# More of layer 1 by seven products: three units of group 7 and four of group 8 in an attention and squared-ReLU kernel

## The chip, the cores and the metric

The kernel runs on one core of a Trainium2 chip. A core has a matrix engine (TensorE, PE in the profile; its weight loads are listed apart as PEld), a vector engine (VectorE, DVE), a scalar engine (ScalarE, ACT), a general engine (GpSimd, POOL) and SyncE (SP), which here only issues DMA transfers. Operands lie in the on-chip memory in 128 partitions; matmul results lie in PSUM, of which this kernel uses eight banks of 128 x 512 fp32. The metric is the time of one execution in microseconds (us) on the device. The page and the trace show one profiled execution.

## The reference

First an attention with a relative position bias, for 8 batches of 8 heads, 576 positions of 64 numbers:

```
scores = scale * q @ k^T + bias_table[bucket(|i - j|)]   # scale = 1/8
attn   = exp(scores - max) ; attn /= sum(attn) + 1e-9
out    = attn @ v
```

Its output, 4608 tokens of 512 numbers (heads side by side), goes through two layers:

```
h   = maximum(x @ w_in, 0)       # w_in: 512 x 2048
out = (h * h) @ w_out            # w_out: 2048 x 512
```

Inputs and output are fp32. The kernel computes in fp16 with fp32 sums.

## The kernel before

**Staging.** Heads are worked in pairs, 32 in all (pair 4b + hp is batch b, heads 2hp and 2hp + 1). GpSimd issues casting loads of q and k into a ring of five staging buffers (`load_six`, `load_rows`). For the first two batches TensorE transposes them; from batch 2 on SyncE issues DMA transposes into `qt` and `kt` (L910). TensorE makes the scores (`run`, L971), ScalarE their exponentials into one of three buffers `pt` (L984), VectorE multiplies the part near the diagonal by exp(bias) (L710), TensorE multiplies by v (`values`, L736 and L743, into the one PSUM bank of `r_pv`), VectorE normalises into `x` (L757, L762), and `x` is transposed into `xt`, from batch 2 on again by SyncE's DMA (L777).

**The two layers** run on 9 groups (0 to 8) of 512 tokens. Layer 1 of a group has 16 tiles of 128 columns of w_in; a plain tile is four matmuls with 512 columns (`f1`, L1486), a ReLU out of PSUM on ScalarE (L1515) and a square on VectorE into `g` (L1525). Layer 2 (`second`) always goes by seven products of quarter blocks in place of eight: sums of activations (`sums_of_activations`, L1170) and of weights are made beforehand, the products are matmuls with 256 columns (L1215, eight for each half of a product), and the quarters of the output are put together on ScalarE and VectorE (L1249, L1243) and stored by SyncE (L1271). In the instruction stream layer 2 of group g - 1 is laid between layer 1 of group g; at the end layer 2 of group 8 stands alone.

**Layer 1 by sevens.** `by_sevens(g, units, due)` does some of the tiles of groups 7 and 8 in the same manner. One unit u takes four tiles (two of each half of w_in's columns) in seven products in place of eight. Four sums of blocks of `xt` are made once for a group, in staging buffers (`t`, names `qs` and `ks` in the profile). For each unit four sums of blocks of w_in are made, 128 x 512 each (`late_sums`, L1296), and serve both groups. They lie in a buffer of the exponentials, `late["room"]`, taken from the ring of three once the last pair's scores are made. A product is four matmuls with 256 columns (L1370). Its results go through PSUM banks a and d (those of the scores, `r_set`), b (`r_g`) and c (the values' one bank, `r_pv`), where products 5 and 3 of a unit share c. Product 1 is copied out by ScalarE (L1401), products 6, 5, 7, 3 and 4 by an add on VectorE (L1396), product 2 goes through the ReLU straight from the bank (L1401); the other three finished quarters get their ReLU in place (L1410), and all four a square on ScalarE or VectorE (L1419, L1421). Before, `UNITS` gives group 7 one unit and group 8 two, so 12 and 8 tiles stay plain.

**What sets the order.** No engine is programmed directly. `P.add` collects operations with their engines, dependencies, buffers and a due time; `Plan.schedule` then simulates the engines with estimated costs, and of the operations that can start first on an engine it takes the one with the earliest due time. The order so found is the order of each engine's instructions. Engines then run in order and wait on semaphores. The table `DUES` overrides the due times of single operations, by their number in the order of `P.add`. A due time is a priority in the planner's nanoseconds, and the profile's clock runs otherwise. Operations that matter below: 98 is the load of pair 5's q; 240, 242 and 244 are the three loads of pair 15's k, and SyncE's transposition into `kt` waits for all three; 1118 and 1094 are the first two plain tiles of group 2, which wait for `xt` of pairs 8 to 11; 1178 is a run of scores of pair 12, 1229 the second part of pair 13's values; 2033 and 2035 are scores of pair 28. From 2150 on numbers differ between the two kernels, since `by_sevens` makes other numbers of operations.

Of the kernel before, what the change touches and what calls it, by code (L numbers as in the profile page):

```python
# [40 lines left out]
SIX = 2  # L41
V_EARLY, V_HW = 18900.0, 2
LATE2 = 7000
UNITS = {7: 1, 8: 2}
V_AFTER = 8
HALVES, HSTEP, HL1 = 1, 1650.0, (20000.0, 34000.0)

AT = (0, 0.5, 2, 2.5, 4, 5.5, 7)
# [15 lines left out]


DUES = """
0:6314 10:217026 16:13035 20:13348 21:258484 25:16976 56:-3806 60:10549 64:7807 66:10391 72:10797 74:9599
80:12958 82:13335 86:9426 88:22059 90:20784 96:15474 98:18110 100:27635 102:17069 104:20413 106:19133 108:15929
110:20294 112:11373 114:26373 118:23163 120:26863 122:27399 124:27420 126:43949 128:373644 130:37551 132:55933
140:51535 146:53249 148:57194 150:58550 152:59093 154:59407 156:62212 158:60024 162:61598 164:73576 166:62626  # L70
168:69684 170:59456 172:62632 174:65227 176:55548 182:127159 185:61268 197:113382 198:91426 200:94475 202:78241
204:62718 208:77636 228:78221 232:79984 234:88997 236:93444 258:97082 260:107098 264:95693 272:353255 290:132179
294:109389 312:161034 317:126634 462:185572 468:197791 498:216177 504:216419 528:-11357 540:58268 548:290781
552:-273 556:362102 569:117287 570:18693 572:322613 573:269880 577:216286 580:63789 588:19830 590:16140
594:14836 595:13461 604:192461 605:259149 615:250357 618:40193 621:36476 626:164336 627:19259 631:22289
632:61824 637:27216 640:23193 641:22984 642:25439 646:24359 648:23862 654:35487 655:137994 656:25970 657:147534
658:26859 669:32802 670:29693 671:29115 675:26812 678:61416 684:27758 687:32723 692:45873 693:44475 694:33461
700:29155 703:40767 706:43870 707:156896 712:138157 715:49177 721:51431 727:42451 730:41204 733:51304 736:188811
739:160633 741:60556 745:65841 746:65543 750:23359 752:198955 754:252034 755:87356 757:149452 759:161491
764:165691 772:38120 780:31226 786:44132 789:65256 791:41900 794:47703 798:179998 803:183900 804:201524  # L80
806:29768 808:32093 814:128297 817:38985 819:48235 822:13166 831:74297 834:41254 836:42214 847:56558 872:76658
876:81357 881:86779 885:82175 890:132194 892:78033 896:74640 901:77029 905:85179 910:92737 913:136934 921:-441
928:71969 932:86010 949:99012 964:77998 968:82501 971:73188 973:72043 979:88379 993:74328 994:172863 1011:91462
1016:95167 1034:90187 1037:94214 1061:98210 1066:103404 1085:116705 1089:123193 1094:115422 1098:123870
1105:125413 1109:116922 1114:123206 1117:104913 1118:108524 1126:215561 1127:140015 1134:341379 1138:129625
1149:123522 1156:126934 1159:128458 1174:117297 1178:116128 1183:123079 1184:121785 1193:130123 1197:131687
1210:103421 1213:171180 1215:111597 1218:107124 1224:123395 1234:97893 1238:106935 1239:113870 1242:121817
1245:107498 1247:139583 1250:140247 1256:140312 1264:152762 1302:164129 1307:159578 1311:156509 1314:140955
1322:175554 1327:174839 1336:155878 1340:158933 1342:162590 1347:179715 1351:176523 1358:154680 1362:174863
1365:164726 1369:178450 1372:164377 1375:183307 1391:148354 1396:141354 1405:158959 1423:158387 1426:145359  # L90
1428:154083 1460:162604 1493:305936 1511:188689 1515:208724 1518:185439 1520:203719 1524:203903 1527:183718
1531:64671 1534:35571 1535:192349 1540:192734 1544:215992 1547:197129 1549:206804 1552:201055 1553:198295
1560:216382 1567:22170 1571:213455 1575:214781 1579:220037 1582:216714 1585:209292 1589:218699 1604:51306
1609:177927 1612:165312 1615:244855 1616:185704 1636:180272 1639:191978 1641:180694 1668:199141 1673:209138
1676:207232 1684:113822 1687:219314 1700:201270 1701:203032 1703:191761 1708:195625 1724:230338 1733:225496
1736:226874 1737:226114 1740:65884 1747:238275 1753:233568 1762:229606 1766:238797 1773:230961 1777:231038
1784:245369 1788:237869 1795:246877 1798:236767 1817:211479 1818:211996 1836:232334 1849:219048 1852:216620
1854:244560 1857:216881 1881:227052 1884:224715 1886:230825 1887:234567 1889:218551 1895:248220 1896:246247
1916:239890 1932:255715 1937:245391 1946:276466 1950:271723 1957:144182 1961:262946 1966:264120 1969:283402
1970:252823 1973:283834 1975:263020 1986:281169 1997:277541 2001:273225 2008:269557 2011:263820 2030:290375  # L100
2033:300439 2035:288262 2038:298147 2070:215597 2094:283860 2099:280265 2140:278987 2160:322023 2175:327834
2187:203430 2191:314100 2194:95297 2196:320960 2200:327640 2205:312307 2209:311170 2216:306662 2220:44915
2227:316413 2231:323176 2238:310309 2241:322560 2256:323083 2258:322318 2260:298171 2281:330645 2283:323528
2290:323454 2298:283980 2316:319108 2342:324427 2349:318937
"""


# [156 lines left out]
def kernel(  # L264
# [48 lines left out]
    pts, p4s = ([t[:, i, :] for i in range(NPT)] for t in (pt_sb, pm_sb))  # L313
# [22 lines left out]
    r_qk, r_pt, r_x = Ring(NQK, True), Ring(NPT), Ring(NX)  # L336
# [28 lines left out]
    def load(*args, **kw):  # L365
# [29 lines left out]
        due=5,  # L395
# [237 lines left out]
    l_win, l_wout, i_wout = [], [], []  # L633
# [55 lines left out]
    last_scores = []  # L689
# [595 lines left out]
    late = {}  # L1285

    def sum_of_w(i, u):
        return pts[late["room"].slot][:, ts(i - 1, 1024)].rearrange("p (k c) -> p k c", k=2)[:, :, ts(u, 256)]

    def late_sums(n, dst, terms, deps, due, bufs=()):  # L1290

        o, made_ = None, []
        for i, (a, b_, op) in terms:
            o = P.add(
                {"DVE": dve(n, 2.0)},
                lambda i=i, a=a, b_=b_, op=op: io(nc.vector.tensor_tensor(out=dst(i), in0=a(), in1=b_(), op=op)),  # L1296
                deps + [o], bufs, due,
            )
            made_.append(o)
        return made_  # L1300
# [2 lines left out]

    def by_sevens(g, units, due):

        assert max(UNITS.values()) <= 2
        if not late:

            late["room"] = Buf(r_pt)
        c = (g * GT) % XR  # L1310
        assert c + GT <= XR
        wq = lambda i, k, u: w_in_sb[:, 2 * k : 2 * k + 2, 1024 * i + 256 * u : 1024 * i + 256 * u + 256]
        xq = lambda k, j: xt_sb[:, 2 * k : 2 * k + 2, c + HALF * j : c + HALF * j + HALF]
        o_ = 4 * (g - min(UNITS)) - 1
        t = lambda i: stg[(i + o_) // 2][(i + o_) % 2][:, 0:512].rearrange("p (k c) -> p k c", k=2)
# [10 lines left out]
        gb1 = g_bufs[g]  # L1326
        for u in range(units):
            s_ = lambda i, u=u: sum_of_w(i, u)
            if ("ops", u) not in late:
                late["ops", u] = late_sums(  # L1330
                    512, s_,
                    [
                        (1, (lambda u=u: wq(1, 0, u), lambda u=u: wq(1, 1, u), mybir.AluOpType.add)),
                        (2, (lambda s_=s_: s_(1), lambda u=u: wq(0, 0, u), SUB)),
                        (4, (lambda u=u: wq(0, 1, u), lambda s_=s_: s_(2), SUB)),
                        (3, (lambda u=u: wq(0, 0, u), lambda u=u: wq(1, 0, u), SUB)),
                    ],
                    l_win + last_scores, due + 10.0 * u, [late["room"]],
                )
            banks = {"a": Buf(r_set), "b": Buf(r_g), "c": Buf(r_pv), "d": Buf(r_set)}  # L1340
            y = {"u": Buf(r_f), "v": Buf(r_y)}
# [16 lines left out]
            for n, i in enumerate((1, 6, 2, 5, 7, 3, 4)):  # L1358
                bk, left, right, first_ = prod[i]
                st = banks[bk]  # L1360
# [5 lines left out]
                def mul(left=left, right=right, first_=first_, ps=ps):  # L1366
# [9 lines left out]
                o = P.add(  # L1376
                    {"PE": 4 * mm(HALF)}, mul,
                    xt_ready[g] + t_ops + late["ops", u] + (read_of[after_read[i]] if i in after_read else []),
                    [st, gb1, late["room"]], due + (8 * u + AT[n]) * 2000.0, 0.0, "f",
                )  # L1380
                f1_last.setdefault(g, []).append(o)
                to, plus, where = reads[i]
# [82 lines left out]
    def layers(g):  # L1465
# [4 lines left out]
        if g < NG:  # L1470
            g_bufs[g] = Buf(r_gb)
            gb1 = g_bufs[g]
            squares[g] = {nt: [] for nt in range(16)}
            units = UNITS.get(g, 0)
            if g < HALVES:
# [82 lines left out]
    for x in DUES.split():  # L1558
        i, due = x.split(":")
# [34 lines left out]
```

## Time and profile before

| what | value |
|---|---|
| five runs | 368.93, 365.24, 367.34, 366.69, 367.06 us |
| median | 367.06 us |
| the profiled execution | 368.93 us, its span 367.1 us |
| matmuls | 4062, of them 84 in units by sevens |
| first matmul, last engine work | 5.3 us, 364.4 us |
| transfers | 44.29 MB, mean 121 GB/s |

In the profile's lines `f<-xt,w_in_sb` means a result tile and its operands, `x16` a count, `L1486` a line of the kernel. A group's line gives the busy time, the mean of one in ns, and after the bar the idle time of the engine before it with what ended it. A line of the chain gives its start, its length and what ran. A stretch gives its length and then the busy time of PE, PEld, DVE, ACT and POOL, with the granted clock of TensorE, the share of the DMA engines and GB/s. In a list of instructions in order of time, start and length come first, and an idle time before the instruction stands in brackets with its releaser. TensorE's granted clock was 1.00 in all stretches.

### The profile page before, as it was taken

How to read it: one execution, taken by the hardware profiler on the slowest of the kernel's cores; microseconds unless marked ns; L12 is line 12 of the kernel's file. 1: busy time of each engine (PE TensorE's matmuls, PEld its weight loads, DVE VectorE, ACT ScalarE, POOL GpSimd, SP SyncE). 2: the span in 40 equal slices, each digit the busy share in tenths (PEclk: the TensorE clock that was granted, in tenths of full speed). 3: DMA queues.
4: the chain of work that ended last, by engine and by line, in shares of the span. 5: the costliest groups of instructions: out<-in, count | busy, mean ns of one | idle time of the engine just before them, and what ended most of it. 6: DMA issues, size and time to landing. Idle time of an engine off the chain costs nothing.

```text
span 367.1 us, 10232 instructions
## 1 busy us (share of the span) xinstructions
PE 353.7 (96%) x4062; PEld 253.0 (69%) x4062; DVE 269.9 (74%) x622; ACT 260.3 (71%) x385; POOL 188.4 (51%) x345
## 2 busy tenths in 40 slices
PE   3989999999999799999999999999999999999996
PEld 3658787765687357777776666557777788566885
DVE  4888989768965499558596579557767785589683
ACT  4999997488866598688977787883685751567530
POOL 8888389989968869978669755013000000000000
PEclk9999999999999999999999999999999999999999
DMA  9999999999999999999999979125320122000032
GB/s 169 139 149 201 202 168 178 134 173 189 119 134 151 220 132 177 149 187 139 155 125 164 177 130 103 63 52 82 105 63 3 49 77 75 31 29 2 30 114 89
DMA packets 162256, 44.29 MB, mean 121 GB/s; under 512 B 145664, under 2 KB 162208, under 8 KB 162208
## 3 DMA queue, kind: packets, MB, share of 16 engines
q0 software_dynamic: 74208, 14.53, 53.0%
q1 hardware_dynamic: 87696, 28.80, 44.8%
q8 instruction: 32, 0.52, 0.6%
q10 hardware_dynamic: 304, 0.31, 0.3%
q14 instruction: 16, 0.13, 0.1%
HBM read 36.89 MB, written 9.44 MB: 126 GB/s over the span
## 4 chain that ended last, share of the span: by engine, by line
PE 85%; DMA 7%; ACT 3%; issue 2%; DVE 2%; POOL 0%; ACTq 0%; SPq 0%
PE f L1215 28%; PE f L1486 26%; PE pv L743 9%; PE st L971 7%; PE f L1439 4%; PE pv L736 3%; DMA xt<-x 2%; DMA kt<-ks 2%; PE st L997 2%; PE st L1022 2%; DMA qs<-in_q_dram 2%; PE st L1370 1%; DMA g<-c_rep 1%; PE f L927 1%; ACT rt L1515 1%
## 5 line engine op out<-in xcount | busy, mean ns | idle before, releaser
L984 ACT ACTIVATE pt<-st 128x1024 f16<-128x1024 f32 x112 | 108.6, 1023 | 25.2 <-PE st L971 25.2
L1486 PE MATMUL f<-xt,w_in_sb 128*128 128x512 f16 (+4 forms) x592 | 113.9, 333 | 2.1 <-DMA xt<-x 2.1
L1515 ACT ACTIVATE rt<-f 128x512 f16<-128x512 f32 x116 | 68.2, 606 | 34.5 <-PE f L1486 31.2
L1486 PEld LDWEIGHTS <-w_in_sb 128*128 128x128 f16 x592 | 51.8, 98 | 44.6 <-issue 12.1
L710 DVE TENSOR_TENSOR pt<-pt,tb_sb 128x512 f16<-128x512 f16 (+3 forms) x108 | 61.6, 583 | 18.1 <-ACT pt L984 16.8
L1525 DVE TENSOR_TENSOR g<-rt 128x512 f16<-128x512 f16 x116 | 51.3, 448 | 28.6 <-ACT rt L1515 27.1
L1215 PEld LDWEIGHTS <-g 128*128 128x128 f16 x576 | 54.6, 98 | 9.0 <-issue 2.1
L349 POOL DMA_DIRECT2D ks<-in_k_dram x79 | 55.9, 720 | 7.2 <-DMA kt<-ks 3.9
L349 POOL DMA_DIRECT2D qs<-in_q_dram x79 | 55.5, 712 | 4.1 <-DMA qt<-qs 2.7
L743 PE MATMUL pv<-va,pt 128*128 128x65 f16 x1280 | 54.6, 193 | 0.0
L743 PEld LDWEIGHTS <-pt 128*128 128x128 f16 x1280 | 50.2, 97 | 2.6 <-issue 0.6
L1215 PEld LDWEIGHTS <-s 128*128 128x128 f16 x432 | 40.9, 98 | 9.4 <-issue 4.2
L1243 DVE SCALAR_TENSOR_TENSOR y<-f,y 128x512 f32<-128x512 f32 (+1 forms) x47 | 31.3, 666 | 18.6 <-PE f L1215 16.4
L1215 PE MATMUL f<-wt,g 128*128 128x256 f16 x288 | 36.2, 273 | 0.0
L954 POOL COPY qz<-qt 64x64 f16<-64x64 f16 x56 | 17.9, 319 | 35.2 <-DMA qt<-qs 30.0
L736 PE MATMUL pv<-vm,pm 128*128 128x130 f16 x160 | 35.4, 221 | 0.4 <-DVE x L762 0.4
L1215 PE MATMUL f<-w_out_sb,s 128*128 128x256 f16 x288 | 35.8, 273 | 0.0
L971 PE MATMUL st<-qt,kt 64*128 64x512 f16 x224 | 33.9, 381 | 0.1
L1215 PE MATMUL f<-w_out_sb,g 128*128 128x256 f16 x272 | 33.3, 273 | 0.0
L762 DVE TENSOR_TENSOR x<-pv,r 128x384 f16<-128x384 f32 (+1 forms) x64 | 31.1, 486 | 1.1
L954 POOL COPY qz<-kt 64x64 f16<-64x64 f16 x56 | 21.1, 376 | 10.4 <-DMA kt<-ks 4.5
L1170 DVE TENSOR_TENSOR s<-g,s 128x1024 f16<-128x1024 f16 x36 | 24.6, 687 | 0.1
(101 smaller groups left out, 410.9 us busy)
## 6 DMA issues: line engine op xcount, KB each, us to landing
out_dram<-y SPq DMA_DIRECT2D x34, 256.0 KB, 2.7
f<-in_v_dram SPq DMA_DIRECT2D x24, 256.0 KB, 4.7
ks<-in_k_dram POOLq DMA_DIRECT2D x48, 64.0 KB, 5.1
qs<-in_q_dram POOLq DMA_DIRECT2D x48, 64.0 KB, 4.5
w_in_sb<-in_moe_w_in_dram POOLq DMA_DIRECT2D x4, 512.0 KB, 8.9
w_out_sb<-in_moe_w_out_dram POOLq DMA_DIRECT2D x4, 512.0 KB, 12.8
ks<-in_k_dram POOLq DMA_DIRECT2D x7, 144.0 KB, 4.8
qs<-in_q_dram POOLq DMA_DIRECT2D x7, 144.0 KB, 5.5
```

What stands on the lines that cost most here:

```text
L349: lambda: io(eng.dma_start(out=out_(), in_=in_())),
L710: io(nc.vector.tensor_tensor(out=a, in0=a, in1=t, op=MULT))
L736: nc.tensor.matmul(ps[:, i, :, :], pm[:, c : c + 128], vm[:, hp, :, 0:65], start=True, stop=False)
L743: nc.tensor.matmul(ps[:, i, e, :], pt[:, (2 * jt + e) * S + c : (2 * jt + e) * S + c + 128], va[:, jt, 2 * hp + e, 0:65], start=False, sto ...
L954: io(eng.tensor_copy(out=dst[qb.slot][rw, rw], in_=src[qb.slot][rw, 512:576]))
L971: nc.tensor.matmul(sets_ps[st.slot][:, e, :], kt[rw, ts(jt, 128)], qt[rw, 0:512], start=True, stop=True,)
L984: nc.scalar.activation(out=p5(pts[pb.slot])[:, jt, :, 0:512], in_=sets_ps[st.slot], func=EXPF, scale=SCALE)
L1215: nc.tensor.matmul(home[bf.slot][:, ts(s_, HALF)], left(c, s_), right(c), start=(c == 0 and (s_ == 0 or apart) and (own or i not in before ...
L1243: nc.vector.scalar_tensor_tensor(out=dst, in0=ps, scalar=OSC, in1=ys[y[plus].slot][:, cs], op0=MULT, op1=mybir.AluOpType.add,)
L1486: nc.tensor.matmul(g_ps[bank.slot][:, a:z], w_in_sb[:, kk, ts(nt, 128)], xt_sb[:, kk, c : c + z - a], start=(kk == 0), stop=(kk == 3),)
L1515: io(nc.scalar.activation(out=rts[rb.slot], in_=g_ps[bank.slot], func=RELUF))
L1525: nc.vector.tensor_tensor(out=gs[gb1.slot][:, nt, :], in0=rts[rb.slot], in1=rts[rb.slot], op=MULT)
```

## The change

`UNITS` becomes 3 for group 7 and 4 for group 8. Group 7 keeps 4 plain tiles, group 8 none. Since a buffer of the exponentials has room for the sums of two units, `by_sevens` takes a second one for units 2 and 3; each unit's sums and products name the room of its pair of units. The sums of units 0, 1 and 2 are now made in group 7's call, those of unit 3 in group 8's. The table of due times is replaced whole: 369 entries before, 407 after, 271 numbers in both.

```diff
-UNITS = {7: 1, 8: 2}
+UNITS = {7: 3, 8: 4}
...
-80:12958 82:13335 86:9426 88:22059 90:20784 96:15474 98:18110 100:27635 102:17069 104:20413 106:19133 108:15929
...
-204:62718 208:77636 228:78221 232:79984 234:88997 236:93444 258:97082 260:107098 264:95693 272:353255 290:132179
...
-1016:95167 1034:90187 1037:94214 1061:98210 1066:103404 1085:116705 1089:123193 1094:115422 1098:123870
-1105:125413 1109:116922 1114:123206 1117:104913 1118:108524 1126:215561 1127:140015 1134:341379 1138:129625
-1149:123522 1156:126934 1159:128458 1174:117297 1178:116128 1183:123079 1184:121785 1193:130123 1197:131687
...
-2033:300439 2035:288262 2038:298147 2070:215597 2094:283860 2099:280265 2140:278987 2160:322023 2175:327834
...
+62:2550 64:8438 66:10313 72:11673 74:9688 80:13143 82:13878 86:9063 88:22768 90:22033 96:14893 98:16878
+100:27518 102:16143 104:21298 106:19938 108:15518 110:20673 112:12408 114:24018 118:23393 120:25313 122:26048
...
+224:80823 226:82118 232:80198 238:89360 240:102185 248:79548 272:114280 280:100590 315:105196 380:132130
...
+1089:120669 1094:116281 1098:124916 1105:126024 1106:127920 1108:102699 1109:118659 1114:121637 1117:105997
+1118:115418 1127:131252 1137:111596 1145:133367 1148:113447 1149:123947 1152:114544 1156:127111 1159:129421
+1178:117144 1183:123401 1184:125052 1186:114321 1197:132662 1206:94845 1210:103572 1215:111049 1218:106871
+1224:122501 1229:119522 1243:120869 1247:137326 1250:140324 1256:144888 1302:162213 1307:160803 1311:157524
...
+2011:265340 2033:262802 2035:268045 2044:275820 2076:261902 2094:280562 2097:270160 2099:277583 2102:275597
...
     def sum_of_w(i, u):
-        return pts[late["room"].slot][:, ts(i - 1, 1024)].rearrange("p (k c) -> p k c", k=2)[:, :, ts(u, 256)]
+        room = pts[late["room", u // 2].slot][:, ts(i - 1, 1024)]
+        return room.rearrange("p (k c) -> p k c", k=2)[:, :, ts(u % 2, 256)]
...
     def by_sevens(g, units, due):
 
-        assert max(UNITS.values()) <= 2
-        if not late:
-
-            late["room"] = Buf(r_pt)
+        for u in range(units):
+            if ("room", u // 2) not in late:
+                late["room", u // 2] = Buf(r_pt)
...
-                    l_win + last_scores, due + 10.0 * u, [late["room"]],
+                    l_win + last_scores, due + 10.0 * u, [late["room", u // 2]],
...
-                    [st, gb1, late["room"]], due + (8 * u + AT[n]) * 2000.0, 0.0, "f",
+                    [st, gb1, late["room", u // 2]], due + (8 * u + AT[n]) * 2000.0, 0.0, "f",
```

## The prediction

> **What bounds the kernel now.** I read the page first (busy time, then the chain that ended last), then the busy time in stretches, the chain in the last 65 us, the groups of the vector and scalar engines there, and at the end the waits of TensorE and SyncE's queue.
>
> ```profile
> PE 353.7 (96%) x4062; PEld 253.0 (69%) x4062; DVE 269.9 (74%) x622; ACT 260.3 (71%) x385; POOL 188.4 (51%) x345
> PE 85%; DMA 7%; ACT 3%; issue 2%; DVE 2%; POOL 0%; ACTq 0%; SPq 0%
> 120.00:140.00 20.00, 18.47 (x159) 9.35 (x159) 14.08 (x33) 16.54 (x26) 15.37 (x27) 1.00 1.46 179
> 270.00:310.00 40.00, 40.00 (x467) 31.41 (x466) 28.48 (x65) 22.78 (x32) 0.00 (x0) 1.00 0.17 46
> 310.00:348.00 38.00, 38.00 (x273) 26.42 (x271) 28.55 (x58) 23.31 (x42) 0.00 (x0) 1.00 0.09 29
> ```
>
> TensorE is the bound: 85% of the chain, and not idle at all from 140 us until its last matmul. The third and fourth numbers of a stretch are PE and PEld, the next two the vector engine (DVE) and the scalar engine (ACT). In 310 to 348 us, where groups 7 and 8 do the layer 1 that the change touches, DVE has 9.5 us free and ACT 14.7. The 1.5 us missing in 120 to 140 us belong to a wait that is shown below. So time comes off the end only as matmuls go away, or as one of TensorE's few waits does.
>
> ```profile
> 313.05 1.73 PE f L1486 x8
> 330.38 0.87 PE st L1370 x8
> L1370 PEld LDWEIGHTS <-pt x48: 97/98/98, 318.7 to 347.9; 128*128 128x128 f16 x48
> L1515 ACT ACTIVATE rt<-f 128x512 f16<-128x512 f32 x20 | 11.8, 595 | 15.4 <-PE f L1486 14.3 <-DVE g L1525 0.7 <-DVE y L1396 0.3
> L1525 DVE TENSOR_TENSOR g<-rt 128x512 f16<-128x512 f16 x20 | 8.3, 422 | 6.0 <-ACT rt L1515 5.7
> L1396 DVE SCALAR_TENSOR_TENSOR rt<-st,y 128x512 f16<-128x512 f32 x3 | 2.1, 686 | 0.0
> L1401 ACT ACTIVATE f<-st 128x512 f32<-128x512 f32 x3 | 1.8, 590 | 0.0
> L1410 ACT ACTIVATE rt<-rt 128x512 f16<-128x512 f16 x7 | 4.4, 623 | 2.7 <-DVE rt L1396 2.7
> L1419 ACT ACTIVATE g<-rt 128x512 f16<-128x512 f16 x7 | 4.4, 630 | 0.2
> L1296 DVE TENSOR_TENSOR pt<-w_in_sb x4: 395/417/419, 272.8 to 280.4; 128x512 f16<-128x512 f16 x4
> ```
>
> **The change, part by part.** The sums go against the profiled execution: 368.93 us, its span of 367.1 and 1.8 around it. That is 1.9 above the median of the five runs (367.06), so I apply the same differences to the median.
>
> *Matmuls.* A plain unit is four tiles of four 512-column matmuls: 16 at 1.73/8 = 0.216 us, 3.46 us. By sevens it is 28 matmuls of 256 columns at 0.87/8 = 0.109: 3.05 us. Four more units: 4 x 0.41 = 1.66 us less on TensorE, all on the path, since nothing else bounds it there. That the smaller matmul pays for its weights is excluded by the third line above: a load takes 98 ns, the matmuls still start 109 ns apart, so loads run under matmuls.
>
> Here a rule speaks against the change. The Trainium skill (TensorE: Matmul & The Clock Gate, "The mechanism") lists that a weight load overlaps matmuls in flight only where the row group differs; these loads all take the full 128 rows. By that rule the 12 more loads of a unit would stand open, 12 x 98 ns, 4.7 us for four units, and the change would lose 3.0. The row above disagrees (the same section also speaks of a background weight buffer), and I go by the row.
>
> *Evictions.* Each unit drops four ReLUs (0.595, ACT) and four squares (0.422, DVE). It adds on DVE five adds at 0.686 (3.43 us), on ACT one copy 0.590, one ReLU from the bank 0.60 and three in place at 0.623 (3.06), and four squares on either engine (0.63 or 0.42). For four units in 300 to 350 us: DVE goes from 35.9 busy (the sum of its ten-microsecond stretches) by -6.8 and +13.7 to 42.8 without squares and 49.6 with all 16; ACT from 25.7 by -9.5 and +12.2 to 28.4, or 38.5 with all squares. The stretch shrinks to 48.3. So if ACT takes most squares (it took seven of ten in this stage) both fit and the cost is 0; if DVE took all, it would be 1.3 over. Ends 0 and +1.3. I take +0.2, near the first, by that share and because back-to-back adds start closer than they last (347.45, 348.06, 348.65 us).
>
> *Sums of w_in.* Units 2 and 3 need eight more sums of 0.417, 3.3 us on DVE. The stretch 270 to 310 leaves DVE 11.5 us, and their room, a second exponentials' buffer, is free once a pair's values are done. Cost 0; without that cover they would stand before the first products of unit 2 and cost up to 3.3. Unit 1's sums only move from group 8's call to group 7's.
>
> *The end of layer 1.* The last product of group 8 goes matmul, add, ReLU, square, and then group 8's layer 2 may start. Before, the last product began at 347.63, its square ended at 351.24 and layer 2 began at 351.56, with 0.3 to spare, TensorE busy with group 7's layer 2 meanwhile. With four units in a row two or three such chains queue. Ends 0 (cover kept) and +1.4 (two more adds of 0.69 in front). I take +0.2, near the row.
>
> *The table of due times.* It is new from end to end. Set against the order in which the trace has the same operations (those below 2150 are the same in both kernels), most new entries repeat that order; up to some 60 us nearly all queues stand as before. The last batch's attention is reordered: pair 28's scores (2033, 2035) get 262802 and 268045 for 300439 and 288262, so values that ran at 301 to 306 us come some 20 us sooner. TensorE is full on both sides of that move, so it costs nothing; it frees the exponentials' buffers sooner and takes normalising off DVE in the last stage.
>
> One place is not neutral:
>
> ```profile
> 116.41 0.60 PE L971 MATMUL st<-qt,kt 64*128 64x512 f16 x4
> 118.14 0.22 PE L736 MATMUL pv<-vm,pm 128*128 128x130 f16 x1
> 118.66 0.81 PE L1486 MATMUL f<-xt,w_in_sb 128*128 128x512 f16 x3
> 121.53 2.75 PE L1486 MATMUL f<-xt,w_in_sb 128*128 128x512 f16 x12 [2.06 <-DMA xt<-x]
> 110.01 1.22 SPq L910 DMA_TRANSPOSE kt<-ks  x1
> 111.94 2.90 SPq L777 DMA_TRANSPOSE xt<-x  x2
> 113.63 7.86 DMA xt<-x
> ```
>
> TensorE waits 2.06 us for the transposed activations of pair 11, which sit on SyncE's queue behind pair 15's k and take 7.86 us to land. The new table puts a score (1178) and values (1229) that ran just before, 0.54 and 0.60, behind the first of these tiles (1118: 115418, against 117144 and 119522): if the transfer lands as before, TensorE arrives 1.14 earlier and waits that much more. But it also puts one load of pair 15's k (240) from the head of the queue to 102185 (it was issued at 83.5 us); then the k transposition is not ready at its old place, the activations go ahead of it, 1.3 us sooner (1.22 and its gap), and pair 15's scores at 130 us have time. Arrival 1.14 earlier and landing 1.3 to 2 earlier nearly cancel. Ends -2.06 (the wait gone) and +1.14. I take -0.3, nearest to the cancelling.
>
> Here the Trainium skill (DMA: Bandwidth & Descriptors, "Issuing engines are not separate DMA queues") says that transfers of all issuing engines share the same 16 DMA engines. The run agrees: q0 and q1 together fill 97.8% of them. So a landing also moves with every load that the table shifts, and the ends stay in the range.
>
> In the first 40 us four GpSimd loads stand 0.3 to 0.6 us earlier by the table, one of them (98) the load for which TensorE waits 0.61 us at 24.12. Ends -0.6 and +0.6 (as much later); I take 0.
>
> **Sum.** -1.66 + 0.2 + 0.2 - 0.3 = -1.56: 367.4 for the profiled execution, 365.5 for the median.
>
> **Rivals.**
> 1. *The gain is waited away at 121 us.* The transfer lands as before: -1.66 + 1.14 + 0.4 = -0.1, 366.9. For it: the row, and that its neighbours landed late too (the k transposition 4.2, the v load between them 7.1 us after issue). Against: the moved k load.
> 2. *The values' one bank bounds the last stage; slower.* Products 5 and 3 of each unit share it, from product 5's start to the end of product 3's add. In before it was held from 344.14 to 349.33, 5.2 us, and 333.25 to some 339.4, 6.1. Seven holds now go one after another into about 38 us: from 5.4 us each it decides. At 5.8 it gives 40.6 - 38 = 2.6 us more than before, 369.7. For it: the third hold, on a busy DVE, was 5.2. Against: the parts alone are 0.44 + 0.69 twice, and the first unit's 13 us was no need but order.
> 3. *Waits go too.* The wait at 121 us and that at 24 vanish: -1.66 - 2.06 - 0.6 + 0.4 = -3.9, 363.1. For it: both loads are moved the right way. Against: DMA is near full there.
>
> **How the numbers follow.** Forecast 0.50, own range 364.3 to 366.8 (+/-1.2 from the terms' ends). Rival 1 0.20, rival 2 0.14, rival 3 0.13, rest 0.03. Half a per cent, 1.84 us, is about what this kernel's runs can tell from nothing (they spread from 365.24 to 368.93); it lies at 365.22. Faster beyond it: half of the forecast's 0.50 less a little (0.22), rival 3 (0.13), a little of rival 1 (0.03): 0.38. Slower: rival 2 and some rest, 0.16. Same: 0.46. The range leaves out most of rival 3's far side and of rival 2's: 363.8 to 368.9.
>
> **What would show it.** Right: L1486's 512-column matmuls fall by 64 and L1370's rise from 84 to 196, at 109 ns; TensorE without idle from 140 us to its end; layer 2 of group 8 starting 1.3 to 2 us sooner. The wait for xt near 121 us tells the forecast from rivals 1 and 3. Wrong: idle TensorE in 310 to 350 us released by L1396 or L1421, or the last matmuls of group 8's layer 2 no sooner than before.

## The result and the profile after

The changed kernel takes 365.49 us (median of 45 runs, 363.44 to 368.05), the kernel before 366.38 (median of 87, 364.89 to 369.17). The ratio is 0.9974, with a 95% interval of 0.9963 to 0.9985: 0.95 us faster (0.55 to 1.36), a gain that is real and lies inside the half per cent that the prediction called "same". The forecast of 365.5 us met the time itself. But it was reached by taking 1.56 from 367.06, and that median of five runs stood 0.7 above the median of 87: so the right time is in part luck, and of the difference 0.6 us is missing. The rest of this document is about where it went.

One caution for reading traces: the profiled execution of before (368.93 us) was 2.5 us above its median, that of after (365.40) is close to its own. Their difference is not the change's.

First the busy time and the chain of after, from the page:

```profile
PE 351.2 (97%) x4110; PEld 256.9 (71%) x4110; DVE 279.5 (77%) x642; ACT 268.2 (74%) x399; POOL 188.1 (52%) x343
PE 84%; DMA 5%; POOL 4%; ACT 3%; DVE 3%; issue 2%; SPq 0%
```

The matmuls are 48 more (64 of 512 columns gone, 112 of 256 come), TensorE's busy time is 2.5 us less, and GpSimd, which was at 0% of the chain, is at 4%. The stretches of after, with the columns as before (length, PE, PEld, DVE, ACT, POOL, granted clock, DMA share, GB/s):

```profile
120.00:140.00 20.00, 20.00 (x209) 11.30 (x208) 15.92 (x38) 17.90 (x28) 14.76 (x27) 1.00 1.68 169
180.00:200.00 20.00, 19.18 (x233) 13.22 (x232) 16.35 (x37) 14.96 (x22) 16.83 (x31) 1.00 1.72 150
270.00:310.00 40.00, 40.00 (x449) 31.66 (x447) 32.20 (x77) 21.87 (x35) 0.00 (x0) 1.00 0.18 50
310.00:348.00 38.00, 38.00 (x346) 33.67 (x345) 33.61 (x58) 30.29 (x54) 0.00 (x0) 1.00 0.11 36
```

The idle time at 120 to 140 us is gone. The stages of the last 160 us keep TensorE full, with VectorE now at 33.6 of 38 us where it was at 28.6. And a stretch that the prediction never looked at, 180 to 200 us, has 0.8 us of idle TensorE.

The end of layer 1 in after, from the lists of instructions of VectorE and TensorE:

```profile
344.13 0.68 DVE L1400 SCALAR_TENSOR_TENSOR rt<-pv,f 128x512 f16<-128x512 f32 x1
344.73 1.28 DVE L1400 SCALAR_TENSOR_TENSOR rt<-st,f 128x512 f16<-128x512 f32 x2
347.18 0.41 DVE L1425 TENSOR_TENSOR g<-rt 128x512 f16<-128x512 f16 x1
348.12 1.91 PE L1219 MATMUL f<-w_out_sb,g 128*128 128x256 f16 x16
```

The last square ends at 347.59 and layer 2 of group 8 begins at 348.12, 0.5 us later and with TensorE busy on group 7 in between. Lines of the changed kernel are four higher than before (L1486 is L1490, L954 is L958).

The place of the new loss, first TensorE's list of after, then GpSimd's:

```profile
193.66 1.46 PE L1490 MATMUL f<-xt,w_in_sb 128*128 128x512 f16 x6
195.49 0.42 PE L1026 MATMUL st<-qt,qz 128*128 128x288 f16 x2 [0.37 <-POOL qz L958]
196.36 0.38 PE L1001 MATMUL st<-qz,kt 128*128 128x128 f16 x4 [0.45 <-DMA f<-in_v_dram]
```

```profile
188.54 2.13 POOL L353 DMA_DIRECT2D ks<-in_k_dram  x3
190.71 0.23 POOL L958 COPY qz<-kt 64x64 f16<-64x64 f16 x1
190.88 2.11 POOL L353 DMA_DIRECT2D qs<-in_q_dram  x3
192.96 2.14 POOL L353 DMA_DIRECT2D ks<-in_k_dram  x3
195.15 0.29 POOL L958 COPY qz<-kt 64x64 f16<-64x64 f16 x1
195.49 0.81 POOL L958 COPY qz<-qt 64x64 f16<-64x64 f16 x2
196.36 0.62 POOL L958 COPY qz<-kt 64x64 f16<-64x64 f16 x2
```

Two pieces of scores wait on `qz`, small copies of `qt` and `kt` that GpSimd makes (L958), 0.82 us in all. They stand behind six load issues, 0.71 us each, 190.88 to 195.10. The second wait carries the name of a load of v; the two `qz` copies before it were done at 196.30 (195.49 and 0.81), so it is those that it waited for, as a run below confirms. In before the same copies stood ahead of their loads, on GpSimd:

```profile
192.37 0.23 POOL L954 COPY qz<-kt 64x64 f16<-64x64 f16 x1
192.66 0.51 POOL L954 COPY qz<-qt 64x64 f16<-64x64 f16 x2
193.21 0.51 POOL L954 COPY qz<-kt 64x64 f16<-64x64 f16 x2
193.78 0.23 POOL L954 COPY qz<-qt 64x64 f16<-64x64 f16 x1
193.95 2.12 POOL L349 DMA_DIRECT2D qs<-in_q_dram  x3
```

The old table holds back two load operations there, 462 with due time 185572 and 468 with 197791. The new table has no entry for either. That became the theory: the units and the last stage give all that was forecast, or a little more, and the two lost entries give about 1 us back at 195 us. The rivals: the units themselves give less (evictions, the end of layer 1, the values' bank), or the new table is worse in some other place.

### The profile page after: what moved, and what is told of

Its sections match the earlier page's. It is cut to its first block, busy times and chain, and to the rows that moved or that the text cites. A ratio compares the mean times of both kernels' runs of the same rounds, so it can differ in the third digit from the quotient of the medians.

```text
span 363.6 us, 10367 instructions
## 1 busy us (share of the span) xinstructions
PE 351.2 (97%) x4110; PEld 256.9 (71%) x4110; DVE 279.5 (77%) x642; ACT 268.2 (74%) x399; POOL 188.1 (52%) x343
## 4 chain that ended last, share of the span: by engine, by line
PE 84%; DMA 5%; POOL 4%; ACT 3%; DVE 3%; issue 2%; SPq 0%
PE f L1219 29%; PE f L1490 21%; PE pv L747 9%; PE st L975 7%; PE f L1443 4%; PE st L1374 3%; PE pv L740 3%; DMA va<-in_v_dram 2%; PE pv L1374 2%; PE st L1026 2%; PE st L1001 2%; POOL va L353 1%; DMA f<-in_v_dram 1%; DMA g<-in_k_dram 1%; ACT pt L988 1%
## 5 line engine op out<-in xcount | busy, mean ns | idle before, releaser
L1490 PE MATMUL f<-xt,w_in_sb 128*128 128x512 f16 (+4 forms) x528 | 98.3, 328 | 0.0
L1519 ACT ACTIVATE rt<-f 128x512 f16<-128x512 f32 x100 | 58.6, 610 | 21.1 <-PE f L1490 18.6
L1490 PEld LDWEIGHTS <-w_in_sb 128*128 128x128 f16 x528 | 45.6, 98 | 36.5 <-issue 8.9
L1529 DVE TENSOR_TENSOR g<-rt 128x512 f16<-128x512 f16 x100 | 42.4, 433 | 19.7 <-ACT rt L1519 18.4
L958 POOL COPY qz<-qt 64x64 f16<-64x64 f16 x57 | 20.1, 352 | 35.0 <-DMA qt<-qs 20.7
L761 DVE RECIPROCAL r<-pv 128x6 f32<-128x6 f32 (+1 forms) x64 | 11.8, 184 | 16.9 <-PE pv L747 16.2
```

The costliest lines, as they stand in the source:

```text
L1490: nc.tensor.matmul(g_ps[bank.slot][:, a:z], w_in_sb[:, kk, ts(nt, 128)], xt_sb[:, kk, c : c + z - a], start=(kk == 0), stop=(kk == 3),)
L1519: io(nc.scalar.activation(out=rts[rb.slot], in_=g_ps[bank.slot], func=RELUF))
L1529: nc.vector.tensor_tensor(out=gs[gb1.slot][:, nt, :], in0=rts[rb.slot], in1=rts[rb.slot], op=MULT)
```

## Experiments

Each ratio is to the kernel before, timed beside it on the same chip.

**Units with the old table up to the last stage.** The changed kernel, but operations below 1300 have their old due times (462 and 468 among them), the rest the new ones.

```diff
-62:2550 64:8438 66:10313 72:11673 74:9688 80:13143 82:13878 86:9063 88:22768 90:22033 96:14893 98:16878
...
+82:13335 86:9426 88:22059 90:20784 96:15474 98:18110 100:27635 102:17069 104:20413 106:19133 108:15929 110:20294
...
+312:161034 317:126634 462:185572 468:197791 498:216177 504:216419 528:-11357 540:58268 548:290781 552:-273
...
```

> The changed kernel (three and four units) with the new table from operation 1300 on, and the old table below, so that the first 120 us and GpSimd's loads stand as in the kernel before. Theory: the matmuls give their whole 1.6 us and nothing is waited away in the last stage; TensorE waits for xt near 121 us as before, and the new wait near 195 us (scores behind copies on GpSimd) is gone: 1.6 us faster than before, ratio 0.9956. Rival (the units themselves give only what the changed kernel shows, the rest goes to adds and ReLUs in the last stage): 0.9 us faster, ratio 0.9975.

Measured: 364.58 us against 366.46, ratio 0.9933 (0.9907 to 0.9960). The rival's 0.9975 is excluded: the loss is not in the units or the last stage. There is no wait at 195 us, and none at 121 us either, where the theory expected that of the kernel before.

**The new table alone.** The kernel before, units 1 and 2, with the new due times for all operations below 2150.

```diff
...
-1105:125413 1109:116922 1114:123206 1117:104913 1118:108524 1126:215561 1127:140015 1134:341379 1138:129625
...
+226:82118 232:80198 238:89360 240:102185 248:79548 272:114280 280:100590 315:105196 380:132130 528:34973 539:46297
...
+1105:126024 1106:127920 1108:102699 1109:118659 1114:121637 1117:105997 1118:115417 1127:131252 1137:111596
...
```

> The kernel before (one and two units) with the new due times for all operations below 2150. TensorE's work is that of before. Theory: the wait for xt near 121 us goes and a wait of about 1 us near 195 us comes; where the first is as long in most executions as in the profiled one, 1.0 us faster (0.9973); where it is usually short, up to 0.7 us slower (1.002), which is what the sum of units and table must give to make the 0.95 us measured. Rival (the table does nothing for the time): 0.9995 to 1.0005.

Measured: 366.96 against 366.46, ratio 1.0015 (0.9995 to 1.0035). If anything the table costs time (0.55 us, -0.2 to 1.3), the second of the two cases that the theory allowed. Its trace has no wait at 121 us and has the wait for `qz` again; of TensorE's waits in this kernel:

```profile
PE f L1486 <- DMA xt<-x: 0.7, 1, 0.7
PE st L997 <- DMA f<-in_v_dram: 0.4, 1, 0.4
PE st L997 <- POOL qz L954: 0.2, 1, 0.2
```

Columns: total us, times, longest. The first is at 157 us and does not stand in the changed kernel's trace.

**The copies ahead of the loads.** The changed kernel with five instructions placed elsewhere in the order and nothing else; 474 is the first load operation of the second group of six issues.

```diff
-    for op in P.schedule():
+    order = P.schedule()
+    moved = [P.ops[i] for i in [1667, 1696, 1697, 1698, 1699]]
+    order = [op for op in order if op not in moved]
+    at = order.index(P.ops[474]) + 0
+    order[at:at] = moved
+    for op in order:
```

> The changed kernel with five copies into qz and kz on GpSimd (operations 1667 and 1696 to 1699, for the scores that TensorE waits for near 195 us) put ahead of six load issues instead of behind them; nothing else moves. Theory: the two waits at 195.5 and 196.4 us go, 1.0 us faster than the changed kernel, 1.9 faster than before, ratio 0.9947. Rival (those waits are of the profiled execution only, or the next late thing takes their place): as the changed kernel, 0.9974.

Measured: 364.51 against 366.46, ratio 0.9935 (0.9910 to 0.9961), an interval that lies wholly below that of the changed kernel. In its list for GpSimd the copies are made at 189.57 and TensorE has its scores at 195.28 without a wait:

```profile
187.42 2.10 POOL L353 DMA_DIRECT2D ks<-in_k_dram  x3
189.57 0.62 POOL L958 COPY qz<-kt 64x64 f16<-64x64 f16 x2
190.25 0.72 POOL L958 COPY qz<-qt 64x64 f16<-64x64 f16 x2
191.03 0.51 POOL L958 COPY qz<-kt 64x64 f16<-64x64 f16 x2
191.48 2.11 POOL L353 DMA_DIRECT2D qs<-in_q_dram  x3
195.28 0.41 PE L1026 MATMUL st<-qt,qz 128*128 128x288 f16 x2
```

**The two entries put back.** The changed kernel with two more entries in its table.

```diff
...
-224:80823 226:82118 232:80198 238:89360 240:102185 248:79548 272:114280 280:100590 315:105196 380:132130
-528:34973 539:46297 540:53567 543:58725 548:8583 556:10502 560:11253 569:15224 570:13674 572:18408 576:8662
...
+226:82118 232:80198 238:89360 240:102185 248:79548 272:114280 280:100590 315:105196 380:132130 462:185572
+468:197791 528:34973 539:46297 540:53567 543:58725 548:8583 556:10502 560:11253 569:15224 570:13674 572:18408
...
```

> The changed kernel with two entries of the old table put back (462:185572 and 468:197791, two loads of q and k on GpSimd that the old table held back and the new one does not). Nothing else in the table moves. Theory: these two entries are what kept the copies ahead of the loads; the waits at 195 to 196 us go, and the time is that of the run with the copies ahead, 1.0 us faster than the changed kernel, ratio to before 0.9947. Rival (it needs the copies themselves moved): as the changed kernel, 0.9974.

Measured: 364.51 against 366.40, ratio 0.9935 (0.9912 to 0.9958); no wait at 195 us. So both repairs of the same place, by order and by due time, give the same 1.0 us by the medians (1.4 by the ratios); the idle time that the trace of the changed kernel showed there was 0.82. Both beat both kernels.

**The table with the two entries, without the units.** The second experiment plus 462 and 468; the one line of the table in which the two differ is shown. With it all four corners of units and entries are measured. (The "fifth experiment" of its expectation is the run with the two entries put back.)

```diff
-226:82118 232:80198 238:89360 240:102185 248:79548 272:114280 280:100590 315:105196 380:132130 528:34973 539:46297
+226:82118 232:80198 238:89360 240:102185 248:79548 272:114280 280:100590 315:105196 380:132130 462:185572 468:197791 528:34973 539:46297
```

> The kernel before (one unit and two) with the new table for operations below 2150 and the two entries 462 and 468 put back, so that the second experiment and this one differ in these two entries alone, and this one and the fifth experiment in the units and the last stage. Theory (units and entries add: units -1.9 us, the two missing entries +0.5 to +1.0, all else in the table 0): 365.9 to 366.5 us, ratio to before 0.999 to 1.001, 0.5 to 1.0 us faster than the second experiment, and no wait for the rearranged copies near 195 us. Rival (other entries of the new table gain or lose as well, and hide in the units' figure): the ratio lies beyond 0.9975 or 1.0025.

Measured: 365.82 against 366.29, ratio 0.9985 (0.9972 to 0.9998). No wait at 195 us. The four corners:

| ratio to before | entries missing | entries there |
|---|---|---|
| one unit and two | 1.0015 (0.9995 to 1.0035) | 0.9985 (0.9972 to 0.9998) |
| three units and four | 0.9974 (0.9963 to 0.9985) | 0.9935 (0.9912 to 0.9958) |

Times 366.4 us and with the half-widths added in squares: the missing entries cost 1.1 +/- 0.9 us with few units and 1.4 +/- 0.9 with many; the units with the last stage give 1.5 +/- 0.8 and 1.8 +/- 1.0; what is left of the new table gives 0.55 (0.1 to 1.0). Along one edge, -0.55 + 1.1 - 1.5 = -0.95, the result. The theory missed narrowly, always to the faster side: 365.82 where 365.9 to 366.5 was expected, 0.9985 where 0.999 to 1.001 was, 1.1 us from the second experiment where 0.5 to 1.0 was. So its statement that all else in the table is worth 0 did not quite hold; the rival's bound, 0.9975, was not reached either.

**Is the gain at 121 us the transfer's?** The prediction's step there was that the transposition of pair 15's k goes behind `xt`. This kernel is before with that one instruction moved on SyncE's queue.

```diff
+    moved = [P.ops[i] for i in [1268]]
+    order = [op for op in order if op not in moved]
+    at = order.index(P.ops[1078]) + 1
+    order[at:at] = moved
```

> The kernel before with one instruction moved: SyncE's transposition of pair 15's k (operation 1268) behind the transposition of pair 11's activations (1078). Theory: the activations are issued about 1.3 us sooner and land sooner by as much, TensorE's wait near 121 us falls from 2.1 to 0.8 us or less, 0.5 to 1.3 us faster, ratio 0.9965 to 0.9986. Rival (the landing is set by the full DMA engines, not by the place in the queue): the wait stays, ratio 1.000.

Measured: 366.47 against 366.46, ratio 1.0005 (0.9980 to 1.0030). In its list for SyncE's queue, and TensorE's:

```profile
109.94 2.58 SPq L777 DMA_TRANSPOSE xt<-x  x2
119.44 3.62 PE L1486 MATMUL f<-xt,w_in_sb 128*128 128x512 f16 x16
```

The second of the two was issued at 111.26 and landed at 115.80, and no wait is left at the tiles. The mechanism is there and the time isn't: the interval leaves at most 0.7 us for it. The rival's ratio came, without its reason, since the wait did not stay.

**Before once more.** The same kernel, unchanged, profiled a second time.

> The kernel before, unchanged, for a second profile. Theory (the 2.1 us wait for xt near 121 us belongs to the slow execution that was profiled first, 368.93 us): no wait of over 0.5 us there, span near 364.6. Rival (the wait is usual, and the moved transposition failed to remove it): 1 to 2.5 us again.

Measured: 367.18 us in one run. From its lists:

```profile
111.77 2.60 SPq L777 DMA_TRANSPOSE xt<-x  x2
119.34 3.62 PE L1486 MATMUL f<-xt,w_in_sb 128*128 128x512 f16 x16
```

The queue runs as in the first execution (there it was issued at 111.94), but here the transfer landed at 118.90, 0.44 before TensorE came. The wait of 2.06 us was that of one execution, a transfer that took 7.86 us where this one took 5.7. (The span, 365.3 us, was not as short as the theory said.) The first experiment, which keeps the old due times there, had no such wait either.

**How near the vector engine is to being the bound.** Two kernels repeat adds of the changed kernel in place: the add of product 7 of each unit (seven more adds), and those of products 7, 3 and 4 (21 more). They write the same result a second time; nothing is left out. Since a repeated add also reads its PSUM bank once more, it keeps that bank longer too; these runs do not separate the two effects.

```diff
...
-                        io(
-                            nc.vector.scalar_tensor_tensor(
-                                out=dst, in0=ps(), scalar=1.0, in1=at(plus), op0=MULT, op1=mybir.AluOpType.add
+                        for _ in range(2 if rb and plus == "v" else 1):
+                            io(
+                                nc.vector.scalar_tensor_tensor(
+                                    out=dst, in0=ps(), scalar=1.0, in1=at(plus), op0=MULT, op1=mybir.AluOpType.add
+                                )
...
+                        for _ in range(2 if rb else 1):
```

> The changed kernel with the add of product 7 of each unit issued twice with the same operands and result, seven more adds, 4.8 us at 0.686. The vector engine was busy 42.7 of 50 us from 300 to 350 us. Theory (7.3 us free, evictions cost nothing): up to 0.5 us slower than the changed kernel, ratio to before 0.9974 to 0.999. Rival (the last stage is already bound by the adds): 3 to 5 us slower, ratio 1.006 to 1.011.

> The changed kernel with the adds of products 7, 3 and 4 of each unit issued twice, 21 more adds, 14.4 us at 0.686 or 12.6 at 0.60 apart. Theory: the 7.3 us that are free are used up and the vector engine becomes the bound of the last stage: 4 to 7 us slower than the changed kernel, ratio to before 1.008 to 1.017. Rival (the adds run beside the matmuls with room to spare): under 2 us slower, ratio below 1.003.

Measured: 367.06 us, ratio 1.0006 (0.9976 to 1.0037), and 375.29 us, ratio 1.0224 (1.0166 to 1.0282): 1.6 and 9.8 us above the changed kernel's median (by the ratios 1.2 +/- 1.2 and 9.2 +/- 2.2). Neither size had been foretold: the first lies between the two expectations, the second above 4 to 7 us. Seven adds are 7 x 0.685 = 4.8 us, of which by the medians 3.2 were absorbed, with VectorE at 9.6 to 9.9 of 10 us from 320 to 350; 21 are 14.4, of which 4.6 were. The stretches of the second kernel, columns as above:

```profile
310.00:320.00 10.00, 8.18 (x71) 6.65 (x69) 9.14 (x16) 6.19 (x11) 0.00 (x0) 1.00 0.00 0
320.00:330.00 10.00, 8.84 (x79) 7.62 (x79) 9.69 (x17) 7.05 (x12) 0.00 (x0) 1.00 0.25 81
330.00:340.00 10.00, 8.92 (x79) 7.41 (x77) 9.86 (x17) 8.07 (x16) 0.00 (x0) 1.00 0.07 23
340.00:350.00 10.00, 9.12 (x80) 7.58 (x78) 9.86 (x18) 5.45 (x10) 0.00 (x0) 1.00 0.02 6
```

and its waits of TensorE there (total us, times, longest):

```profile
PE st L1374 <- DVE rt L1401: 3.6, 7, 0.8
PE pv L1374 <- DVE rt L1401: 1.6, 3, 0.7
```

With VectorE at 9.7 to 9.9 of 10 us, the products wait for the banks that its adds have not yet read, those of the scores twice as much as the values' one. The same stretches of the changed kernel:

```profile
320.00:330.00 10.00, 10.00 (x94) 8.97 (x92) 9.34 (x16) 8.18 (x14) 0.00 (x0) 1.00 0.22 75
330.00:340.00 10.00, 10.00 (x94) 8.97 (x92) 8.96 (x16) 9.44 (x19) 0.00 (x0) 1.00 0.09 29
340.00:350.00 10.00, 10.00 (x94) 8.95 (x93) 9.50 (x18) 5.74 (x11) 0.00 (x0) 1.00 0.16 54
```

By these runs it has some three to five us to spare, and not the 7.3 that 50 - 42.7 of busy time would suggest.

**One unit more.** Four units for both groups, so that no plain tile is left in group 7, with the copies ahead of the loads and due times of its own in the last stage.

```diff
-UNITS = {7: 3, 8: 4}
+UNITS = {7: 4, 8: 4}
...
```

> An eighth unit: group 7 gets four units as well, so no plain tile is left in it; copies ahead of the loads as in the third experiment, and due times of the last stage of its own. Theory (the vector engine has some 3 us left in the last stage, by the experiments that doubled adds; the eighth unit brings it five more adds, 3.4 us, against 0.41 us less of matmuls): no gain over the kernel with the copies ahead, 364.2 to 365.2 us, ratio to before 0.994 to 0.997, and the vector engine above 9.3 of 10 us busy in most stretches of 310 to 350 us. Rival (matmuls still bound alone): 0.4 us faster than that kernel, 364.1 us, ratio 0.992 to 0.993, with the vector engine below 9 of 10.

Measured: 364.14 against 365.86, ratio 0.9958 (0.9939 to 0.9976). The ratio is the theory's and the median the rival's (0.4 us below that of the kernel with the copies ahead, 364.51); a ratio this wide cannot tell 0.4 us. And the theory's reason is not in the trace: VectorE is above 9.3 in one stretch only (9.56 in 320 to 330, else 9.10 to 9.22), since the due times let it begin sooner, and TensorE is full from 300 to 360 us. From the first tile of layer 1 to its last matmul TensorE is busy for 328.1 us in this trace and for 329.0 in that of the copies ahead, which speaks for a gain, as far as two single executions go. What an eighth unit is worth stays open.

## Why the prediction was right, and where it was not

The time came out, and so did the likeliest outcome, a change of less than half a per cent. By its steps:

**Matmuls, -1.66: held.** The counts are those foretold (512-column matmuls 336 to 272 in the trace, by sevens 84 to 196), at 109 ns:

```profile
338.08 0.60 PE L1374 MATMUL pv<-xt,pt 128*128 128x256 f16 x4
338.52 1.04 PE L1219 MATMUL f<-w_out_sb,s 128*128 128x256 f16 x8
339.39 0.60 PE L1374 MATMUL st<-xt,w_in_sb 128*128 128x256 f16 x4
```

Four begin 0.44 us before the next, eight 0.87. The traces agree: from TensorE's first tile of layer 1 (30.48 us in before, 30.49 in after) to its last matmul it was busy for 330.65 us in before and 329.00 in after, 1.65 less. The units and their last stage give 1.5 +/- 0.8 and 1.8 +/- 1.0; with the old table below operation 1300, and so with the rest of the new table, it is 1.9 by the medians (2.5 +/- 1.0 by the ratio). The rule on weight loads that the prediction weighed (Trainium skill, TensorE: Matmul & The Clock Gate, "The mechanism") would have made this part lose 3.0 us; that is excluded.

**Evictions, +0.2, and the end of layer 1, +0.2: 0 in the profile.** TensorE has no idle time from 200 us to its last matmul. ScalarE took 21 of the 28 squares, as its share before suggested; VectorE had 42.66 us of 300 to 350 against 42.8 forecast without squares; so near an agreement is partly chance, for it did seven squares there, four more than before (some 1.6 us), while the normalising that was 1.3 us there before is gone. Layer 2 of group 8 starts 3.4 us sooner by the two traces. Since the first tile of layer 1 TensorE waited 2.82 us in before and 1.02 in after (the 2.06 at 121 us gone, the 0.82 at 195 us new), so 1.8 of it is waiting and 1.6 is left, within the 1.3 to 2 foretold, as far as two single executions go. These two terms were cautious by 0.4 us in all, which the ratios cannot tell from right; the doubled adds show that the caution was not idle, since only some half of VectorE's apparent room could be used.

**Sums of w_in, 0, and the last batch's attention, 0: held.** TensorE is full over 270 to 310 us, with VectorE at 32.2 of 40; the last values run at 287 us in place of 306.

**The first 40 us, 0: held.** The wait for pair 5's q was 1.20 us in after and 0.61 in before, but its matmul starts at 24.14 and 24.12, and the first tile of layer 1 at 30.49 and 30.48.

**The wait at 121 us, -0.3.** Of the two changes that were to cancel, the landing won: the two transfers into `xt` were issued from 108.47 on with the k transposition behind them, as foretold, and the second landed at 114.73 in place of 121.49. That is 6.8 us sooner and not the "1.3 to 2" of the prediction: 3.5 by its issue (110.09 for 113.63) and 3.2 by its way (4.6 us for 7.86). (Operation 1118's due time in the new table is 115417, not the 115418 given there; it stays ahead of 117144.) In after, SyncE's queue:

```profile
108.47 2.85 SPq L781 DMA_TRANSPOSE xt<-x  x2
111.41 0.53 SPq L353 DMA_DIRECT2D f<-in_v_dram  x1
112.03 1.23 SPq L914 DMA_TRANSPOSE kt<-ks  x1
```

But the wait that this removed was not usual. It was one execution's, and the kernel with the transfer alone moved gains nothing that shows. The 97.8% by which the prediction took the DMA engines for filled is the packets' time as an average of the whole span; the share was 1.46 in 120 to 140 us and 0.17 in 270 to 310, so it does not say what held this transfer. The rest of the table gives 0.55 (0.1 to 1.0), of which 0.3 would be a fair part; which of its places gives it was not found.

**The table's other places: the step that failed.** The prediction wrote "One place is not neutral" and looked for it where the profile of before had a wait. The place that counted had none before: GpSimd's queue at 190 to 195 us, where two entries, 462 and 468, are not changed but dropped. All the entries that the prediction names are ones that the new table has; it names none that the table lacks. That cost 1.1 to 1.4 us: with -0.55 for the rest, the table comes to +0.55, where -0.3 was forecast. So the difference to before is -0.95 and not -1.56. The time agreed because the five runs' median was 0.7 high by chance, which made up for it.

**The rivals.** Rival 1 (waited away at 121 us) is out by the traces, which have no wait there; a form of it is what happened, at another place and by another engine. Of rival 3 the wait at 121 us is gone and the one at 24 us is not, and its time, 363.1 us, is excluded. Rival 2 set its point at 5.4 us per hold of the values' bank. From product 5's start to the end of product 3's add the seven holds of after are 6.5, 3.7, 5.3, 6.6, 4.0, 3.5 and 4.1 us: 4.8 in the mean, 33.7 of 39 us. The mean did not reach it, though two holds did, and TensorE did not wait. Where the doubled adds make it wait, it is for the banks of the scores first.

## What to carry to other kernels

When a table of priorities or a schedule is replaced, compare the keys that vanish as well as those that are new, and read the order on every queue that mixes transfers' issues with work that the bound engine waits for; a place without a wait in the trace before is where a wait can be added. Profile the kernel before twice before pricing a wait on a transfer. Here busy time overstated an engine's room: repeating one of its instructions and timing that gives an idea of how much is left.

## What the runs showed of the hardware

A load issue held GpSimd's queue for 0.71 us (2.13 for three), against 0.23 us for the shortest of the copies, so six issues delayed the copies behind them by 4.3 us. The Trainium skill (DMA: Bandwidth & Descriptors, "SWDGE vs HWDGE vs iDMA") says that for transfers that GpSimd issues, its own cores work out the descriptors. That this fills the 0.71 us no run here shows.

The same transposing transfer, at the same place of the same queue, took 5.7 us to land in one execution of before and 7.86 in another; with k's transposition behind it it took 4.5 (the kernel with that one instruction moved) and 4.6 (after). A landing time read from one profile is good to about 2 us here.
